# Gate row moved to the head of ScalarE's load queue, first value part placed ahead of x1's transposes, one dummy matmul pair fewer

## The chip, the core and the metric

The kernel runs on one core of one Trainium2 chip. The metric is device time in microseconds of one launch, from the runs of the kernel: three runs before the change, of which the median counts. The profile shows one further execution, taken by the hardware profiler.

## What is computed

A gated mix of a linear attention (hedgehog features) and a SwiGLU feed-forward block, both fed from the same x of 2048 tokens by 640 columns, in bf16:

```python
def reference(A_x, A_wqkv, A_w_phi, A_wo, B_x, B_w_gate, B_w_up, B_w_down, gate_w):
    def _A_ref(x, wqkv, w_phi, wo):            # 32 heads of 20 columns
        qkv = (x @ wqkv).reshape(B, S, 3, H, Dh).transpose(2, 0, 3, 1, 4)
        q, k, v = qkv[0], qkv[1], qkv[2]
        pq = jnp.einsum("bhsd,hdf->bhsf", q, w_phi)
        pk = jnp.einsum("bhsd,hdf->bhsf", k, w_phi)
        phi_q = jnp.concatenate([_softmax(pq), _softmax(-pq)], axis=-1)
        phi_k = jnp.concatenate([_softmax(pk), _softmax(-pk)], axis=-1)
        kv = jnp.einsum("bhsf,bhsd->bhfd", phi_k, v)
        z  = jnp.einsum("bhsf->bhf", phi_k)
        num = jnp.einsum("bhqf,bhfd->bhqd", phi_q, kv)
        den = jnp.einsum("bhqf,bhf->bhq", phi_q, z)[..., None] + 1e-6
        return (num / den).transpose(0, 2, 1, 3).reshape(B, S, D) @ wo
    def _B_ref(x, w_gate, w_up, w_down):
        return (_silu(x @ w_gate) * (x @ w_up)) @ w_down
    x = A_x
    g = _sigmoid((x * gate_w).sum(-1, keepdims=True))
    return g * _A_ref(x, A_wqkv, A_w_phi, A_wo) + (1 - g) * _B_ref(x, B_w_gate, B_w_up, B_w_down)
```

The part that matters here is the start: the values v = x @ wqkv[:, 1280:1920], to which the gate's column is joined (gate_w becomes the 641st column of the value weights, so that the gate's logit falls out of the same matmuls).

## The kernel before

The tokens are cut into 16 tiles of 128 (t = 0 to 15), the 640 columns of x into 5 chunks of 128. Two strings set everything: LOADS (line 33) is the order in which the transfers from HBM are issued, ORDER (line 38) the order in which the work is handed to the engines. Each word is one item, run by the table at line 952. Each engine then works through its own list in order; a wait on another engine or on a transfer is a semaphore wait that the tracker (line 145) puts in front of an instruction. An instruction that waits holds up all that stands behind it on its engine, and a transfer is issued by the engine in whose list it stands (SP or ScalarE, shown as SPq and ACTq in the profile).

The items of the head, in the names of the strings:

- x0 to x3 load the first four tiles of x as rows (128 x 640, 160 KB, into xs); XQ at line 391 gives x0 to SP and x1, x2, x3 to ScalarE.
- w0 to w4 load the five row chunks of the value weights (128 x 640 each, 160 KB, into wvg); WQ at line 392 gives w0 and w4 to ScalarE, w1, w2, w3 to SP.
- g loads the gate row gate_w as five rows of 128 into gwr (line 414, on SP). It waits for the memset that clears gwr on GpSimd (line 431).
- f0, k0 and further words load weights on SP.
- H (warm, line 511) is a pair of dummy matmuls of 128x128 on a constant, which need no data. ORDER starts with 13 of them.
- X0.0 transposes chunk 0 of x0 on TensorE into PSUM and lets VectorE copy it to xT; X0.1 does so for the other four chunks, with the copy on ScalarE. X1, X2, X3 transpose whole tiles, all copied on VectorE.
- G (gcol, line 505) turns the five gate rows into five columns on TensorE, and VectorE casts them into column 640 of wvg.
- U t.c (vpart, line 539) is chunk c of the values of tile t: two matmuls of 320 and 321 columns with wvg's chunk c, which add up over c in one PSUM pair of banks. The last, c = 4, hands the pair to ScalarE (v_out).
- h loads w_phi on ScalarE after a wait on w3.

PSUM has four pairs of banks. next_pair (line 489) gives an item the pair that was used longest ago and is not held; a pair handed out again is written only when its last reader is done. Every H, too, takes a pair. From the item I to the item N the pair 3 is out of this ring, since it collects the key-value sums.

After the head, TensorE runs value tiles (V), feature premultiplication of the weights (M), key tiles (K), key-value sums (E), query tiles (Q), feed-forward items (F), output of the attention (O) and the down projection (D).

Of the kernel before, what the change touches and what calls it, by code (L numbers as in the profile page):

```python
# [6 lines left out]
P = 128  # L7
# [23 lines left out]


LOADS = """
x0 w0 x1 g w1 x2 w2 x3 w3 w4 f0 k0 k1 t4 k2 k3 k4 k5 t5 t6 t7 t8 t9 t10 t11 t12 t13 t14 t15 q0 q1 q2 q3 q4 q5
 f1 f2
"""

ORDER = """
H0 H1 H2 H3 H4 H5 H6 H7 H8 H9 H10 H11 H12 X0.0 G X0.1 X1 h U0.0 U1.0 U0.1 X2 U1.1 U2.0 U0.2 U1.2
U2.1 X3 U2.2 U0.3 U1.3 U2.3 U0.4 U1.4 U2.4 V3 Y i4 F0.1 M0 M1 F0.2 M2 V4 M3 M4 F0.0 M5 K0 i3 K1 S0 I  # L40
P0 K3 S1 P1 F1.0 K2 V6 E0 V8 K4 S2 S3 E1 S4 K5 S5 P2 P3 V7 E2 V5 R0 K6 P4 P5 R2 E3 K7 S6 E4 V15 K8
E5 V10 S7 P6 K9 E6 R1 P7 S8 K10 S9 E7 K11 S10 V9 V11 P8 E8 K12 P9 R3 E9 P10 K13 S11 E10 K14 S12 P11
# [11 lines left out]
class _Tracker:  # L54
# [90 lines left out]
    def run(self, eng, fn, reads=(), writes=(), dma=False):  # L145
        rkeys = list(dict.fromkeys(k for a in reads for k in self.keys_of(a)))
        wkeys = list(dict.fromkeys(k for a in writes for k in self.keys_of(a)))
        need = {}

        def req(ev, raw):  # L150
            if ev is None:
                return
            s, v = ev
            if s == eng and not dma and (eng == "pe" or not raw):
                return
            if v > need.get(s, 0):
                need[s] = v

        for k in rkeys:
            for kk in self._conflicts(k):  # L160
                req(self.lastw[kk], True)
                if k[0] == "psum":
                    for s, v in self.readers[kk].items():
                        req((s, v), False)
        for k in wkeys:
            for kk in self._conflicts(k):
                req(self.lastw[kk], True)
                for s, v in self.readers[kk].items():
                    req((s, v), False)
        self._wait(eng, need)  # L170
        ins = fn()
        if dma:
            sn = "d%d" % self.ndma
            self.ndma += 1
            self._add_sem(sn)
            inc = 16
        else:
            sn, inc = eng, 1
        ins.then_inc(self.sem[sn], inc)
        self.cnt[sn] += inc  # L180
        v = self.cnt[sn]
        snap = dict(self.known[eng])
        if not dma:
            snap[sn] = max(snap.get(sn, 0), v)
        self.evknow.setdefault(sn, {})[v] = snap
        ev = (sn, v)
        for k in wkeys:
            self.lastw[k] = ev
            self.readers[k] = {}
        for k in rkeys:  # L190
            r = self.readers[k]
            if r.get(sn, 0) < v:
                r[sn] = v
        return ev


def _build(nc, A_x, A_wqkv, A_w_phi, A_wo, B_x, B_w_gate, B_w_up, B_w_down, gate_w, out):
    tr = _Tracker(nc)
    pe, act, dve, pool, sp = nc.tensor, nc.scalar, nc.vector, nc.gpsimd, nc.sync
# [3 lines left out]
    def sb(name, shape, dtype):  # L203
        t = nc.alloc_sbuf_tensor(name, list(shape), dtype)
        tr.reg(t, "sbuf", nc.lookup_mloc(t).addr)
        return t
# [94 lines left out]
    gwr = sb("gwr", [P, P], BF16)  # L301
# [72 lines left out]
    def dma(e, dst, src, transpose=False):  # L374
        eo = tr.eng[e]

        def fn():
            if transpose:
                return eo.dma_start_transpose(dst, src)
            return eo.dma_start(dst, src)  # L380
        rd = [src] if src.tensor.name in tr.base else []
        wr = [dst] if dst.tensor.name in tr.base else []
        return run(e, fn, rd, wr, dma=True)
# [9 lines left out]
    x2 = A_x[0]  # L393
# [18 lines left out]
        wv_evs.append(load_rows(WQ[c], wvg[:, c, 0:D], c, 2 * D))  # L412

    def load_gate():
        dma("sp", gwr[0:5, :], bass.AP(gate_w.tensor, gate_w.offset, [[P, 5], [1, P]]))

    def load_phi():
        tr._wait("act", dict([wv_evs[3]]))
# [527 lines left out]
    def kv_end():  # L946
# [6 lines left out]
        "H": lambda i: warm(), "i": fills, "X": xpose, "G": gcol, "U": vpart, "V": vtile,  # L953
        "M": lambda m: premult(1, m), "R": lambda m: premult(0, m),
        "K": ktile, "S": knorm, "P": kmul, "p": lambda t: kmul(t, "dve"), "E": kvtile, "x": load_x, "t": load_xt, "w": load_wv, "g": load_gate, "h": load_phi, "k": lambda m: load_wt(1, m), "q": lambda m: load_wt(0, m),
        "f": lambda i: load_ffn(FCUT[i], FCUT[i + 1]), "L": load_late_weights, "T": tail_weights, "J": gates,
        "Y": w_blocks, "I": kv_begin, "N": kv_end, "Z": z_row,
# [51 lines left out]
```

## Time and profile before

| | us |
|---|---|
| median of 3 runs | 285.62 |
| the runs | 285.57, 285.62, 285.80 |
| the profiled execution | 286.04 |
| its span, first to last instruction | 284.8 |

| engine | busy us (share of the span) | instructions |
|---|---|---|
| TensorE matmul (PE) | 281.9 (99%) | 1809 |
| TensorE weight load (PEld) | 156.8 (55%) | 1809 |
| VectorE (DVE) | 193.2 (68%) | 280 |
| ScalarE (ACT) | 139.6 (49%) | 241 |
| GpSimd (POOL) | 155.3 (55%) | 119 |

The profiled execution has 1.2 us outside its span. Busy times of the matmuls are those of a pipeline and overlap: the spacing of their starts, not the length of one, tells how fast TensorE goes. In the timelines each line has the start, the time until the group's end, the engine, the line of the kernel, the operation, output <- inputs, and the number of instructions; in brackets the idle time ahead of the first and what ended it. "ACTq" and "SPq" are the issues of transfers by ScalarE and SP. The granted clock of TensorE is 1.00 in the whole span.

### The profile page before, as it was taken

Reading aid. Unit: us, or ns where it says so; the run is one execution under the profiler, and the core shown is the slowest. Engines: PE = TensorE matmul, PEld = TensorE weight load, DVE = VectorE, ACT = ScalarE, POOL = GpSimd, SP = SyncE. Lnnn points to the kernel's source line nnn. Section 1 sums busy time; section 2 is a strip of 40 time slices with the busy share of each in tenths; the row PEclk is TensorE's granted clock in tenths of the full one; section 3 lists DMA queues with packets and bytes.
Section 4 is the critical chain, followed back from the end, with each engine's and each line's share of the span. In section 5 each row is a group of like instructions: output and inputs, shape, how many; then the busy total and the mean of one; then the engine's idle time right before and its main releaser. Section 6 shows DMA issues by size and latency. Waiting matters only on the chain.

```text
span 284.8 us, 4696 instructions
## 1 busy us (share of the span) xinstructions
PE 281.9 (99%) x1809; PEld 156.8 (55%) x1809; DVE 193.2 (68%) x280; ACT 139.6 (49%) x241; POOL 155.3 (55%) x119
## 2 busy tenths in 40 slices
PE   8999999999999999999999999999999999999997
PEld 6666777766645445445545444554544444444766
DVE  1346667784789998979999899997878355053100
ACT  2477687786755666657746764130101675001022
POOL 6276988888167859597858744463062553100100
PEclk9999999999999999999999999999999999999999
DMA  7986679200065362022330200623547520133411
GB/s 231 232 104 129 109 136 370 86 3 0 3 218 185 78 107 51 9 52 53 60 52 3 52 4 10 138 51 71 115 139 138 76 61 7 41 78 73 122 46 46
DMA packets 62085, 25.19 MB, mean 88 GB/s; under 512 B 51023, under 2 KB 61543, under 8 KB 62063
## 3 DMA queue, kind: packets, MB, share of 16 engines
q1 hardware_dynamic: 60534, 24.03, 37.7%
q10 hardware_dynamic: 1529, 0.87, 1.1%
q8 instruction: 14, 0.23, 0.4%
q14 instruction: 8, 0.07, 0.1%
HBM read 10.16 MB, written 2.63 MB: 45 GB/s over the span
## 4 chain that ended last, share of the span: by engine, by line
PE 98%; DMA 1%; DVE 0%; issue 0%
PE ps L326 97%; DMA xs<-in_A_x_dram 1%; PE ps L338 1%; DVE osb L934 0%
## 5 line engine op out<-in xcount | busy, mean ns | idle before, releaser
L354 POOL TENSOR_TENSOR hT<-hT,us 128x512 bf16<-128x512 bf16 (+1 forms) x37 | 42.9, 1167 | 43.5 <-DVE hT L358 33.2
L326 PE MATMUL ps<-xT,wg 128*128 128x512 bf16 x260 | 64.6, 379 | 0.0
L326 PE MATMUL ps<-xT,wu 128*128 128x512 bf16 x260 | 64.6, 379 | 0.0
L354 POOL TENSOR_TENSOR ph<-eq,qc 128x1320 bf16<-128x1320 bf16 x16 | 40.3, 2521 | 31.0 <-DVE qc L673 19.8
L326 PE MATMUL ps<-wqk,xT 128*128 128x320 bf16 x320 | 47.9, 299 | 0.0
L344 ACT ACTIVATE us<-ps 128x512 bf16<-128x512 f32 (+1 forms) x56 | 33.4, 597 | 22.0 <-PE ps L326 19.8
L326 PEld LDWEIGHTS ps<-xT,wu 128*128 128x128 bf16 x260 | 25.4, 98 | 30.7
L326 PEld LDWEIGHTS ps<-xT,wg 128*128 128x128 bf16 x260 | 25.0, 98 | 28.4 <-ACT oT L344 0.6
L354 POOL TENSOR_TENSOR ekr<-ekr,krec 128x1280 bf16<-128x1280 bf16 x16 | 37.3, 2358 | 5.8 <-DVE krec L368 5.8
L344 ACT ACTIVATE eq<-ps 128x640 bf16<-128x640 f32 x32 | 22.3, 703 | 32.3 <-PE ps L326 31.2
L358 DVE SCALAR_TENSOR_TENSOR hT<-hT,ps 128x512 bf16<-128x512 bf16 (+1 forms) x37 | 25.0, 681 | 19.1 <-ACT hT L344 17.5
L326 PEld LDWEIGHTS ps<-wqk,xT 128*128 128x128 bf16 x320 | 30.4, 98 | 13.3
L354 POOL TENSOR_TENSOR hx<-hx,us 128x512 bf16<-128x512 bf16 (+1 forms) x19 | 24.1, 1272 | 22.1 <-DVE hx L358 16.3
L344 ACT ACTIVATE hT<-ps 128x512 bf16<-128x512 f32 (+1 forms) x37 | 22.0, 596 | 25.0 <-PE ps L326 24.8
L326 PE MATMUL ps<-hT,wd 128*128 128x512 bf16 (+1 forms) x140 | 31.1, 379 | 0.0
L365 DVE TENSOR_REDUCE ksum<-ekr 128x64 f32<-128x1280 bf16 x16 | 23.4, 1464 | 11.0 <-ACT ekr L344 11.0
L344 ACT ACTIVATE ekr<-ps 128x640 bf16<-128x640 f32 x32 | 22.3, 703 | 6.9 <-PE ps L326 6.4
L326 PE MATMUL ps<-wvg,xT 128*128 128x320 bf16 (+1 forms) x160 | 24.7, 305 | 0.0
L365 DVE TENSOR_REDUCE qw<-ez 128x64 f32<-128x1280 bf16 x16 | 23.6, 1476 | 0.0
L365 DVE TENSOR_REDUCE qz<-eq 128x64 f32<-128x1280 bf16 x16 | 23.6, 1478 | 0.0
L354 DVE TENSOR_TENSOR ez<-eq,zb 128x1280 bf16<-128x1280 bf16 x16 | 22.9, 1449 | 0.6 <-DMA zb<-zrow 0.6
L326 PEld LDWEIGHTS ps<-hT,wd 128*128 128x128 bf16 (+1 forms) x140 | 13.0, 97 | 16.1 <-issue 1.3
(103 smaller groups left out, 291.2 us busy)
## 6 DMA issues: line engine op xcount, KB each, us to landing
wd<-in_B_w_down_dram SPq DMA_DIRECT2D x1, 2080.0 KB, 10.3
out_dram<-osb SPq DMA_DIRECT2D x2, 640.0 KB, 3.5
wg<-in_B_w_gate_dram SPq DMA_DIRECT2D x1, 1040.0 KB, 8.6
wu<-in_B_w_up_dram SPq DMA_DIRECT2D x1, 1040.0 KB, 9.8
wog<-in_A_wo_dram SPq DMA_DIRECT2D x2, 375.0 KB, 4.1
wg<-in_B_w_gate_dram SPq DMA_DIRECT2D x1, 640.0 KB, 5.0
wu<-in_B_w_up_dram SPq DMA_DIRECT2D x1, 640.0 KB, 6.3
omgb<-omgd SPq DMA_DIRECT2D x2, 256.0 KB, 4.0
```

The source lines that it names most:

```text
L326: last = pe.matmul(o, lhsT=l, rhs=r, start=st, stop=sp_, skip_group_check=sk)
L338: last = pe.transpose(o, i, ident[0:k, 0:k])
L344: return run("act", lambda: act.activation(o, i, func, scale=scale), rd, [o])
L354: return run(e, lambda: eo.tensor_tensor(o, a, b, op), [a, b], [o])
L358: return run("dve", lambda: dve.scalar_tensor_tensor(out=o, in0=a, scalar=s, in1=b, op0=op0, op1=op1), rd, [o])
L365: return run("dve", lambda: dve.tensor_reduce(o, i, AX.X, ALU.add), [i], [o])
```

## The change

The gate row is issued by ScalarE instead of SP, as the first of its transfers, ahead of w0 and x1. In ORDER the first value part U0.0 goes ahead of X1, and one of the 13 dummy pairs at the start is left out. With one pair taken less from the ring, and U0 taking its pair ahead of X1, the numbers of the PSUM pairs that the later items get are permuted.

```diff
 LOADS = """
-x0 w0 x1 g w1 x2 w2 x3 w3 w4 f0 k0 k1 t4 k2 k3 k4 k5 t5 t6 t7 t8 t9 t10 t11 t12 t13 t14 t15 q0 q1 q2 q3 q4 q5
+x0 g w0 x1 w1 x2 w2 x3 w3 w4 f0 k0 k1 t4 k2 k3 k4 k5 t5 t6 t7 t8 t9 t10 t11 t12 t13 t14 t15 q0 q1 q2 q3 q4 q5
  f1 f2
 """

 ORDER = """
-H0 H1 H2 H3 H4 H5 H6 H7 H8 H9 H10 H11 H12 X0.0 G X0.1 X1 h U0.0 U1.0 U0.1 X2 U1.1 U2.0 U0.2 U1.2
+H0 H1 H2 H3 H4 H5 H6 H7 H8 H9 H10 H11 X0.0 G X0.1 U0.0 X1 h U1.0 U0.1 X2 U1.1 U2.0 U0.2 U1.2
...
     def load_gate():
-        dma("sp", gwr[0:5, :], bass.AP(gate_w.tensor, gate_w.offset, [[P, 5], [1, P]]))
+        dma("act", gwr[0:5, :], bass.AP(gate_w.tensor, gate_w.offset, [[P, 5], [1, P]]))
```

## Prediction

> **What bounds the kernel now.** I read the page's chain first, then the timelines of the first 9 us by engine, then a table of stretches for the matmuls that read wvg.
>
> ```profile
> PE 98%; DMA 1%; DVE 0%; issue 0%
> PE ps L326 97%; DMA xs<-in_A_x_dram 1%; PE ps L338 1%; DVE osb L934 0%
> ```
>
> The chain never leaves TensorE once x0 has landed. So the time is the start of the first transpose, plus TensorE's work, plus whatever gaps and slow matmuls stand among it. Only the head can move.
>
> ```profile
> 3.04 0.74 PE L518 MATMUL ps<-const-bfloat16-1.0 128*128 128x128 bf16 x5
> 3.85 0.29 PE L338 MATMUL ps<-ident,xs 128*128 128x128 bf16 x1
> 4.12 0.19 PE L326 MATMUL ps<-ident,gwr 128*128 128x5 bf16 x1
> 4.17 1.12 PE L338 MATMUL ps<-ident,xs 128*128 128x128 bf16 x9
> 5.08 1.67 PE L326 MATMUL ps<-wvg,xT 128*128 128x320 bf16 x6
> 6.59 0.44 PE L338 MATMUL ps<-ident,xs 128*128 128x128 bf16 x5
> 6.87 1.53 PE L326 MATMUL ps<-wvg,xT 128*128 128x320 bf16 x10
> ```
>
> ```profile
> 3.85 0.10 PEld L338 LDWEIGHTS ps<-ident,xs 128*128 128x128 bf16 x1 [0.35 <-DMA xs<-in_A_x_dram]
> 4.12 0.10 PEld L326 LDWEIGHTS ps<-ident,gwr 128*128 128x128 bf16 x1 [0.16 <-DMA gwr<-in_gate_w_dram]
> ```
>
> TensorE waits twice: for x0 (the 26 dummies are spaced 107 ns, so the last one's 107 ns end near 3.57, and X0.0 starts at 3.85: 0.29 us) and for the gate row (0.16 us). After 4.12 it has no gap in the head.
>
> ```profile
> 5.08:6.42 1.34, 1.34 (x5) 0.70 (x6) 0.00 (x0) 1.00 1.05 350
> 6.87:8.23 1.36, 1.36 (x10) 0.81 (x10) 0.00 (x0) 1.00 1.09 362
> ```
>
> This is the stretch table (stretch, sum, busy and count for TensorE first, then its weight loads). In equal time 5 matmuls of 320 columns start, and later 10: 267 ns each, then 136. The granted clock column says 1.00 in both, so it doesn't show this step. The x6 group at 5.08 is cut short in its last matmul (6.42 to the next start at 6.59, 171 ns), which puts the step near 6.50 us. Before 6.50 a wait costs about half its length: what was not done at 267 ns is done later at 136 (1 - 136/267 is lost, 0.49).
>
> ```profile
> 0.80 0.41 ACTq L380 DMA_DIRECT2D wvg<-in_A_wqkv_dram  x1
> 1.24 1.43 ACTq L380 DMA_DIRECT2D xs<-in_A_x_dram  x3
> 2.70 0.45 ACTq L380 DMA_DIRECT2D wvg<-in_A_wqkv_dram  x1
> 3.19 1.28 ACT L344 ACT_TABLE_LOAD   x1 [3.19 <-issue]
> 4.79 0.60 ACT L344 ACTIVATE xT<-ps 128x512 bf16<-128x512 bf16 x1 [0.33 <-PE ps L338]
> ```
>
> ScalarE issues five loads one after another, then loads its table until 4.47, and the copy of X0.1 follows at 4.79, when its transposes are done: slack 0.32 us.
>
> ```profile
> 0.81 0.39 SPq L380 DMA_DIRECT2D xs<-in_A_x_dram  x1
> 1.26 0.36 SPq L380 DMA_DIRECT2D gwr<-in_gate_w_dram  x1
> 1.66 1.30 SPq L380 DMA_DIRECT2D wvg<-in_A_wqkv_dram  x3
> ```
>
> **The change, part by part.** Gate row at the head of ScalarE's queue: it waits for POOL's memset of gwr (0.80 to 1.00 in the timeline), so it issues near 1.05 and takes 0.36 (its SP row), with 0.03 to the next issue, as between the others. Everything queued behind it on ScalarE moves 0.65 us: w0 from 0.80 to 1.45, x1 from 1.24 to 1.89, x2 to 2.38, x3 to 2.87, w4 to 3.35, and the table load from 3.19 to 3.84. It then ends at 5.12, and the copy of X0.1 runs 5.13 to 5.73 instead of 4.79 to 5.39. Who waits for it: U0.1, which reads the copied columns, and before that U1.0, because the PSUM ring hands U1 the pair that X0 used (before the change and after it, by the order of next_pair calls). A release reaches TensorE about 0.05 us after the end (the copy that ends at 7.08 frees a weight load at 7.13). So U1.0 starts no earlier than 5.78, against 5.62 now (two 267 ns matmuls after 5.08). On SP w1, w2, w3 and the weights behind them issue 0.42 us earlier (1.66 to 1.24), which nothing needs: those land well ahead of their use.
>
> One dummy pair fewer: 24 x 107 ns from 0.84 end near 3.41 (3.57 - 0.21).
>
> x0's landing: its issue-to-landing is 3.0 us (0.81 to 3.81) with w0 beside it, which landed at 4.0 (3.2 after 0.80). The next 160 KB, x1, landed at 4.4 (3.1 after 1.24), so 160 KB are worth some 0.4 us. Without the half of w0 that went ahead of x0's last packets, X0.0 may start near 3.6. Bounds: 3.41 (the dummies' end) and 3.85 (no gain); 3.6 is the middle, taken by the 0.4 us row. The gate row, first on its ring, should land between 1.5 us after 1.05 (the shortest landing of a store on ScalarE's queue, 24 KB) and 2.9 us after (its own wait ending at 4.12, issued 1.26), so 2.6 to 3.95. I take it as hidden; at 3.95 it would still hold TensorE 0.25 us, which the later bound on U1.0 swallows.
>
> U0.0 ahead of X1: X0.0, G and X0.1 take 0.107 + 0.047 + 4 x 0.107 = 0.58, so TensorE is free at 4.18. U0.0 needs VectorE's copy and cast (at 4.18 + 0.22 and 4.35 + 0.18 now, that is 0.67 after X0.0's start, with the hop 0.72: 4.32) and w0: 1.45 + 3.2 = 4.65 by its own row, 4.4 if it is the third 160 KB to land, as x1 is now. It then runs 0.53 us, from 4.45 to 4.98, or 4.7 to 5.23. X1 needs x1: 1.89 + 3.1 = 5.0 by its own row, 1.89 + 4.1 = 6.0 by x2's, which is now issued at 1.73 and has a rival transfer on SP, as x1 will have. I take 5.3, nearer to its own row; X1 then ends at 5.85 and U1.0 starts near 5.87. With x1 at 5.0 it is 5.78, by the ScalarE copy; with 6.0 it is 6.55.
>
> Before and after, the same work stands ahead of U1.0 (X0, G, X1, U0.0). So the whole change is U1.0's start: 5.87 against 5.62, 0.25 us later (0.16 to 0.93). The earlier x0 and the vanished gate wait buy nothing past this point, since the ScalarE copy ends late whatever TensorE does. At half price that is +0.12 us (0.08 to 0.49, the part past 6.50 counted whole).
>
> The later steps keep their cover, if each landing shifts by 0.65: x2 5.8 to 6.5 (X2 then near 6.7), x3 7.0 to 7.7 (X3 8.2), w4 8.0 to 8.7 (U0.4 9.6). The permuted PSUM pairs put F1.0 on K0's pair, whose two exponentials end near 24.1, with F1.0 at 25.15: 1 us of cover.
>
> **Sum.** The profiled execution took 286.04 (284.8 of span, 1.2 around it), the runs' median is 285.62. Span 284.8 + 0.12 gives 284.92, 286.16 for a profiled run and 285.74 against the median.
>
> **The rivals.** First, the step from 267 to 136 ns comes later. TensorE's idle time between the first dummy and the step is 0.29 + 0.16 = 0.45 us now. After, it is 3.41 to 3.6, 4.18 to 4.45, 4.98 to 5.3: 0.78, with 0.95 where x1 is later. For it: 2.73 us of unbroken dummies were not enough now, so the idle parts may count. Against: 0.45 us of gaps didn't prevent the step. Price: the step stands 2.38 us behind the end of the last gap (4.12); from 5.87 that is 8.25, 1.75 us later x 0.49 = 0.86, so 286.6. If the run-up of 5.66 us (0.84 to 6.50) counts from X0.0 at 3.6, it is 9.26, 1.35 us, so 287.1. It decides as soon as the idle share before 6.50 no longer lets the step happen there. [...]
>
> Second, x1 lands as late as x2's row: U1.0 at 6.55, +0.49, and X2 may wait another 0.1 to 0.3: 286.1 to 286.4. For it: transfers are at 339 to 363 GB/s between 5 and 8 us. Against: x1 itself came in 3.1 us.
>
> Third, x0 does not land earlier at all (3.81): U0.0 and X1 then run 0.25 later, but ScalarE's copy still sets 5.78 and x1 5.87: 285.7, no change.
>
> Fourth, faster: the waits can give back at most 0.29 + 0.16 us, halved 0.22, and only if the table load does not shift. More needs the step itself to come earlier, say at 5.0: 1.5 x 0.49 = 0.73, so 285.0. Nothing in the trace speaks for it, except that one execution shows one position of the step.
>
> **How the numbers follow.** 0.2% is 0.57 us, about what a measurement can tell. Forecast 0.38 (no measurable change, its own range 285.4 to 286.1); step later 0.37 (slower, 286.5 to 287.5); late x1 0.08 (0.05 of it beyond 0.2%); no earlier x0 0.04; faster 0.13. So faster 0.13, same 0.38 + 0.03 + 0.04 = 0.45, slower 0.37 + 0.05 = 0.42. The range 285.1 to 287.5 leaves out most of the faster case and the far end of the late step.
>
> **What would show it.** In the changed profile: w0's issue near 1.45 and the table load near 3.84; X0.0 near 3.6; no wait on the gate row; gaps ahead of U0.0 and X1; U1.0 at 5.8 to 5.9, behind ScalarE's copy or x1. The step: count matmuls of 320 columns around 6.5. If they are still at 267 ns past 7 us, the first rival holds and the forecast falls; if U1.0 starts before 5.62, my reading of ScalarE's queue is wrong.

## The result, and the profile after

The changed kernel is slower: 289.58 us median of 6 runs (288.75 to 291.36) against 285.65 us for the kernel before (285.37 to 286.4). The ratio is 1.0137, 95% interval 1.0113 to 1.0161, some 3.9 us. The profiled execution took 289.47 us, with a span of 288.2 us (before: 286.04 and 284.8).

The chain of waits of the changed kernel from 0.80 us on, its first pieces in order of time (start, length, what):

```profile
0.80 0.20 POOL gwr L372
1.00 0.15 POOL ident L372
1.16 0.43 ACTq L380
1.59 0.03 issue
1.62 0.39 ACTq L380
2.01 0.03 issue
2.04 4.65 DMA xs<-in_A_x_dram
```

Before, the chain began with x0's transfer (3.0 us). Now it leads through ScalarE's issues, the gate row's and w0's, to x1, which takes 4.65 us from issue to landing. ScalarE's own timeline shows what stands there:

```profile
1.04 0.55 ACTq L380 DMA_DIRECT2D gwr<-in_gate_w_dram  x1
1.62 0.39 ACTq L380 DMA_DIRECT2D wvg<-in_A_wqkv_dram  x1
2.04 1.41 ACTq L380 DMA_DIRECT2D xs<-in_A_x_dram  x3
3.48 0.65 ACTq L380 DMA_DIRECT2D wvg<-in_A_wqkv_dram  x1
4.16 1.28 ACT L344 ACT_TABLE_LOAD   x1 [4.16 <-POOL v1x L372]
5.46 0.60 ACT L344 ACTIVATE xT<-ps 128x512 bf16<-128x512 bf16 x1
```

w0 is issued at 1.62 instead of 0.80, x1 at 2.04 instead of 1.24. TensorE's timeline of the changed kernel:

```profile
3.35 0.31 PE L338 MATMUL ps<-ident,xs 128*128 128x128 bf16 x1
3.46 0.21 PE L326 MATMUL ps<-ident,gwr 128*128 128x5 bf16 x1
3.53 0.59 PE L338 MATMUL ps<-ident,xs 128*128 128x128 bf16 x4
5.91 0.69 PE L326 MATMUL ps<-wvg,xT 128*128 128x320 bf16 x2 [1.79 <-DMA wvg<-in_A_wqkv_dram]
6.74 0.71 PE L338 MATMUL ps<-ident,xs 128*128 128x128 bf16 x5
7.34 1.25 PE L326 MATMUL ps<-wvg,xT 128*128 128x320 bf16 x4
8.39 0.74 PE L338 MATMUL ps<-ident,xs 128*128 128x128 bf16 x5
8.92 2.88 PE L326 MATMUL ps<-wvg,xT 128*128 128x320 bf16 x10
11.60 0.56 PE L338 MATMUL ps<-ident,xs 128*128 128x128 bf16 x5
```

X0.0 starts at 3.35, right behind the dummies and 0.5 us earlier than before. Then TensorE stands still for 2 us until w0 has landed, and 0.3 us more until x1 has. U1.0 starts at 7.34; before, it was 5.62. And the slow matmuls go on: ten matmuls of a value tile take from 8.92 to 11.60 (268 ns each), where before they took 1.36 us. The table of stretches for the matmuls that read wvg (stretch, sum, busy and count of TensorE, weight loads, VectorE, granted clock, share of the transfer engines, GB/s):

```profile
9.99:11.06 1.07, 1.07 (x5) 0.60 (x4) 0.00 (x0) 1.00 1.06 139
12.00:13.07 1.07, 1.07 (x8) 0.78 (x9) 0.00 (x0) 1.00 1.24 201
```

The five transposes at 11.60 take 0.39 us to the next start (0.53 when slow, 0.28 when fast), so the step from 267 to 136 ns lies near 11.83; before, near 6.50. The granted clock column says 1.00 in both rows and again doesn't show it. The clock records of the trace, which the column is made from, begin only with the step itself: at 11.823 us, and at 6.482 in the kernel before, which agrees with the spacing. Ahead of the first record the column reads 1.00.

In the profiled execution two parts add up to the whole. U1.0 starts 7.34 - 5.62 = 1.72 us later. Behind U1.0 the matmuls stay slow for 11.83 - 7.34 = 4.49 us instead of 6.50 - 5.62 = 0.88; the 3.61 us more cost half, 0.49 x 3.61 = 1.77. Together 3.49 us. TensorE's last matmul starts at 286.13 instead of 282.66, 3.47 later. Past the head nothing moved: from the first feed-forward matmul (15.26, before 11.78) to the last matmul there are 270.87 us, before 270.88. So the permuted PSUM pairs cost nothing.

### The profile page after: what moved, and what is told of

It is laid out like the page before. It is cut to its first block, busy times and chain, and to the rows that moved or that the text cites. A ratio compares the mean times of both kernels' runs of the same rounds, so it can differ in the third digit from the quotient of the medians.

```text
span 288.2 us, 4686 instructions
## 1 busy us (share of the span) xinstructions
PE 283.2 (98%) x1800; PEld 157.3 (55%) x1807; DVE 192.6 (67%) x280; ACT 139.6 (48%) x241; POOL 155.4 (54%) x119
## 4 chain that ended last, share of the span: by engine, by line
PE 97%; DMA 2%; ACTq 0%; issue 0%; POOL 0%; DVE 0%; POOLq 0%
PE ps L326 96%; DMA xs<-in_A_x_dram 2%; PE ps L338 1%; ACTq L380 0%; DVE osb L934 0%; POOL gwr L372 0%; POOL ident L372 0%; POOLq L994 0%
## 5 line engine op out<-in xcount | busy, mean ns | idle before, releaser
L326 PE MATMUL ps<-wvg,xT 128*128 128x320 bf16 (+1 forms) x160 | 26.4, 316 | 1.8 <-DMA wvg<-in_A_wqkv_dram 1.8
L354 DVE TENSOR_TENSOR ez<-eq,zb 128x1280 bf16<-128x1280 bf16 x16 | 22.3, 1408 | 1.1 <-DMA zb<-zrow 1.1
```

The source lines that it names most:

```text
L326: last = pe.matmul(o, lhsT=l, rhs=r, start=st, stop=sp_, skip_group_check=sk)
L354: return run(e, lambda: eo.tensor_tensor(o, a, b, op), [a, b], [o])
```

## The experiments

All kernels were timed beside the kernel before on the same chip; a ratio is to that kernel. Issue and landing times below are those of the trace's transfer records in the one profiled execution of each. The code below is cut to the words that change; "..." stands for what is left out.

### Which part of the change is it

e1 keeps only the gate row's move, e2 only the order on TensorE, e3 only the missing dummy pair.

```diff
# e1: after, with ORDER as before
-H0 ... H11 X0.0 G X0.1 U0.0 X1 h U1.0
+H0 ... H12 X0.0 G X0.1 X1 h U0.0 U1.0
# e2: before, with
-X0.0 G X0.1 X1 h U0.0 U1.0
+X0.0 G X0.1 U0.0 X1 h U1.0
# e3: before, with
-H0 ... H11 H12 X0.0
+H0 ... H11 X0.0
```

> Only the gate row's move to the head of ScalarE's queue, with 13 dummy pairs and X1 ahead of U0.0 as in the kernel before. Theory Q (the move delays w0 and x1, and TensorE's long gap also delays its step from 267 to 136 ns): w0 lands near 5.8 and x1 near 6.7 as in the changed kernel, TensorE has a gap of 2 us or more, time 289 to 291. Theory O (the loss comes from U0.0 being put ahead of X1): 285.5 to 286.2, as before the change.

> Only U0.0 ahead of X1, with the gate row on SP and 13 dummy pairs. Theory Q: w0 lands at 4.0 and x1 at 4.4 as before, gap of some 0.1 us for the cast, time 285.4 to 286.0. Theory O: most of the 3.9 us, 288 or more.

> Only one dummy pair fewer. Theory Q: the gap before X0.0 grows from 0.29 to 0.50 us and nothing else, 285.4 to 286.0. Rival D (the dummies hold the step in place, and a pair fewer delays it by microseconds): 286.5 or more, with 267 ns matmuls past 7 us.

e1: 290.4 us, ratio 1.0147 (1.011 to 1.0185). w0 1.64 to 5.90, x1 2.06 to 6.80, and one gap on TensorE up to 6.85:

```profile
6.85 0.71 PE L338 MATMUL ps<-ident,xs 128*128 128x128 bf16 x5 [2.52 <-DMA xs<-in_A_x_dram]
```

e2: 285.77 us, 0.9991 (0.9972 to 1.0009). e3: 285.7 us, 0.9989 (0.9971 to 1.0007). The gate row's move is the whole loss; the other two parts make no difference that can be measured. Theory O and rival D fall.

### What the slow clock adds

e4 fills the changed kernel's waits with dummy matmuls. e9 and e10 leave all transfers as in the kernel before, and only hold TensorE at U0.0 until 7.5 us, e9 idle, e10 with dummies.

```diff
# e4: after, with b(n) = n dummy matmuls into the PSUM pair of the last H
-X0.0 G X0.1 U0.0 X1 h U1.0
+X0.0 G X0.1 b18 U0.0 b3 X1 h U1.0
# e9: before, with one more memset of GpSimd and j = TensorE's wait on it
+    hold = memset("pool", hT[:, 1, 0:4, :], 0.0)
-X0.0 G X0.1 X1 h U0.0 U1.0
+X0.0 G X0.1 X1 h j U0.0 U1.0
# e10: as e9, with (b into the pair of G)
+X0.0 G X0.1 X1 h b26 j U0.0 U1.0
```

> The changed kernel with 18 dummy matmuls (1.9 us at 107 ns) between X0.1 and U0.0 and 3 between U0.0 and X1, so that TensorE is busy while it waits for w0 and x1. If the late step is made by the gaps, U1.0 stays near 7.4 and the step comes back to 6 to 8 us: 286.8 to 287.8, some 2 us less than the changed kernel. If the step's place has nothing to do with the gaps: 289 to 290, with the step still near 11.8.

> The kernel before with one wait put into TensorE's list ahead of U0.0, on an extra memset of GpSimd that ends near 7.5 us; all transfers and their order as before. So TensorE idles 2.4 us (5.08 to 7.5) with nothing else changed. Theory H (an idle stretch makes the step from 267 to 136 ns come later): step at 9.5 to 12, 288.4 to 289.8, that is 2.4 us of waiting less 0.7 for what would have been slow before 6.5, plus half of the slow time behind 7.5. Rival (the step does not care for the gap): U0.0 on runs at 136 ns, 287.2 to 287.6.

> The same wait to 7.5 us, with 26 dummy matmuls put in front of it, so that TensorE has work in most of it. Theory H: the step stays at 4.5 to 8 and the time is 287.0 to 288.0, some 1 to 2 us below the kernel with the bare gap. Rival: the same time as the bare gap.

e4: 288.4 us, ratio 1.0074 (1.0039 to 1.0108), 1.2 us below the changed kernel by the medians, and above the 286.8 to 287.8 that was expected. In its profile x1 happened to land at 8.16, later than in the changed kernel (6.69), and U1.0 started only at 8.76; the matmuls behind it were fast all the same:

```profile
5.83 0.73 PE L326 MATMUL ps<-wvg,xT 128*128 128x320 bf16 x2
6.37 0.36 PE L529 MATMUL ps<-const-bfloat16-1.0 128*128 128x128 bf16 x3
8.21 0.45 PE L338 MATMUL ps<-ident,xs 128*128 128x128 bf16 x5 [1.47 <-DMA xs<-in_A_x_dram]
8.76 0.72 PE L326 MATMUL ps<-wvg,xT 128*128 128x320 bf16 x4
```

The five transposes at 8.21 already take the fast 0.45. So in this execution the step came early, but the wait was not shorter.

e9: 289.31 us, 1.0123 (1.0106 to 1.0139). e10: 287.73 us, 1.0076 (1.0055 to 1.0098). The wait ends at 7.5 in both; the difference of 1.58 us is what TensorE did meanwhile. The stretch tables, first e9 (stretch, sum, busy and count of TensorE, granted clock, transfer share, GB/s), then e10 (with weight loads and VectorE between, matmuls on wvg only):

```profile
4.68:6.00 1.32, 0.17 (x3) 1.00 0.92 309
6.00:7.00 1.00, 0.00 (x0) 1.00 1.08 367
7.00:7.50 0.50, 0.00 (x1) 0.62 1.06 360
7.50:10.50 3.00, 3.00 (x15) 0.50 1.36 265
10.50:11.00 0.50, 0.50 (x5) 0.96 0.07 19
```

```profile
4.68:7.50 2.82, 0.01 (x1) 0.01 (x1) 0.00 (x0) 1.00 0.98 327
7.50:8.50 1.00, 0.98 (x6) 0.49 (x6) 0.00 (x0) 1.00 1.09 360
```

Here the granted clock does show it: in e9 it falls to 0.50 inside the gap (0.62 over the half microsecond before 7.50 means some 0.38 us of it, so from about 7.12) and stays there until about 10.54. In this execution the step to fast matmuls had already come by 4.4 us, and the idle stretch took it back for 3.4 us; half of that is 1.7 us. In e10 the clock stays at 1.00. All four runs of e9 read a mean granted clock of 0.994 over the kernel, as such a fall gives, and all four of e10 read 1.000. Theory H holds, in this form: here idle time cost twice, as waiting and as slow matmuls afterwards.

The column shows a fall in three profiles, and in each it reads 0.50 for about 3.4 us. By the shares of the stretches in which the falls begin and end, they run from 7.12 to 10.54 in e9, from 7.37 to 10.78 in e13 (0.84 over 6.26 to 7.90, 0.51 over 10.00 to 10.80) and from 7.18 to 10.60 in e7 (0.94 over 6.32 to 7.30, 0.95 over 10.50 to 11.50).

What sets the place of the step in the head isn't shown. In the changed kernel it came 5.08 us after the last wait for a transfer had ended (6.74 to 11.82), in the kernel before 2.36 us after (4.12 to 6.48). In e9, whose head has the loads and the order of the kernel before up to the wait, it came by 4.4 us. Its place differs from execution to execution: the size of the loss in one execution is in part luck.

How much idle time brings a fall isn't settled by these runs. In e7 one followed a wait of 1.45 us, some 0.86 us after the wait's end (6.32 to 7.18):

```profile
6.32 0.45 PE L338 MATMUL ps<-ident,xs 128*128 128x128 bf16 x5 [1.45 <-DMA xs<-in_A_x_dram]
```

```profile
6.32:7.30 0.98, 0.88 (x8) 0.94 1.05 342
7.30:8.30 1.00, 1.00 (x9) 0.50 1.05 366
```

Behind the wait of 1.47 us in e4, and behind one of 1.77 us in e11 below, the matmuls stayed fast.

### Why w0 and x1 land so late

The prediction let a load that is issued 0.65 us later land 0.65 us later, by its own row. e11 tests that in the kernel before, with nothing moved but the start of ScalarE's issues, by 0.38 us. e5 to e8 vary the two queues of the changed kernel, and e13 takes SP's loads away from beside w0.

```diff
# e11: before, with a = ScalarE waits for GpSimd's 2nd memset
-x0 w0 x1 g w1
+x0 a w0 x1 g w1
# e5: after, with the gate row on SP and a = ScalarE waits for GpSimd's 3rd operation
-x0 g w0 x1 w1
+x0 g a w0 x1 w1
# e6: after, with y = a second gate row load on SP, into a scratch tile
+x0 y g w0 x1 w1
# e7: after, with
+x0 w0 g x1 w1
# e8: after, with z = 16 rows of x on ScalarE, into a scratch tile
+x0 z g w0 x1 w1
# e13: after, with a = SP waits for GpSimd's 9th operation (until 3.5 us)
+x0 g w0 x1 a w1
```

> The changed kernel with the gate row back on SP, behind x0, so SP's issues stand as before the change; ScalarE's first load w0 is only held back, by a wait on GpSimd's identity, to about 1.7 us (1.62 in the changed kernel, 0.80 before). Theory L (a late start of ScalarE's loads is enough: their first packets then stall both queues alone, behind x0): w0 lands at 5.3 to 6.0, 288.5 to 291. Theory C (SP's w1 and w2, issued 0.4 us earlier, take the transfer engines from w0): w0 lands at 4.4 to 4.9, 285.8 to 286.8. Theory S (the five small rows at the head of ScalarE's queue do it): as C, 285.8 to 286.8.

> The changed kernel with a second small load on SP behind x0 (the gate row once more, into a scratch tile that nobody reads in time), so that w1, w2, w3 issue at their times of before (1.66, 2.06, 2.53) while ScalarE's queue stays as changed. Theory C: w0 lands at 4.4 to 4.9, 286 to 287. Theories L and S: w0 still at 5.3 to 6.0, 288.5 to 291.

> The changed kernel with w0 first and the gate row second on ScalarE's queue. w0 issues at 0.80 again, x1 near 1.7. Theory L: w0 lands near 4.0 as before, the gate row by 4.2, x1 at 4.6 to 5.2, and time 285.4 to 286.4. Theory S (small rows anywhere ahead of x1 hold the ring): x1 at 6 or later, 287.5 or more.

> The changed kernel with one more load ahead of the gate row on ScalarE's queue: 16 rows of x (20 KB) into a tile not in use yet, issued at 0.80 with no wait. w0 is then issued near 1.8, later still. Theory L in its sharper form (the first packets of a queue are slow on each transfer engine, and the stall falls beside x0's own when the queue starts at 0.80): the stall near 3.0 to 3.7 goes, w0 lands at 4.5 to 5.0, 286.3 to 287.5. If only the time of issue counts: w0 at 5.8 or later, 289 to 291.

> The kernel before, all as it was, but ScalarE's first load held back by a wait on GpSimd's second memset, so that w0 issues near 1.2 instead of 0.80 and x1 near 1.6 instead of 1.24. If a load keeps its 3.2 us from issue to landing (as the prediction had it): w0 4.4, x1 4.7, 285.6 to 286.2. If loads issued by about 1.3 land in the first wave and the later ones only at 5 to 6 us: w0 by 4.5, x1 at 5.0 to 6.3, a gap of 0.5 to 1.5 us ahead of X1, 286.3 to 288.5.

> The changed kernel with SP's loads behind x0 (w1 and all that follow) held back until about 3.5 us, so that w0, issued at 1.6 on ScalarE, has the transfer engines to itself behind x0. If w0 is late because it shares the engines with SP's loads: it lands by 4.4 (its own 3.2 us of before, or less). If a load issued at 1.6 starts slowly whatever runs beside it: 5.0 or later. The total time says little here, since w1 comes late on purpose: 287 to 291.

| kernel | w0 issued, landed | x1 | w1 | median us | ratio (interval) |
|---|---|---|---|---|---|
| before | 0.80, 4.00 | 1.24, 4.38 | 1.66, 4.77 | 285.65 | 1 |
| after | 1.62, 5.78 | 2.04, 6.69 | 1.26, 3.49 | 289.58 | 1.0137 (1.0113 to 1.0161) |
| e5 | 1.70, 5.22 | 2.13, 5.94 | 1.66, 4.98 | 287.76 | 1.0068 (1.0046 to 1.0089) |
| e6 | 1.64, 5.27 | 2.04, 6.01 | 1.66, 5.06 | 289.5 | 1.0112 (1.0046 to 1.0178) |
| e7 | 0.80, 3.92 | 1.86, 6.28 | 1.26, 4.33 | 288.42 | 1.0078 (1.004 to 1.0116) |
| e8 | 1.86, 6.25 | 2.25, 7.12 | 1.26, 3.61 | 288.75 | 1.0112 (1.0085 to 1.0139) |
| e11 | 1.18, 3.54 | 1.60, 5.89 | 1.68, 5.69 | 288.1 | 1.0065 (1.0035 to 1.0095) |
| e13 | 1.63, 4.41 | 2.03, 4.87 | 3.50, 7.85 | 289.13 | 1.0096 (1.006 to 1.0133) |

e11 is the clearest. x1 is issued 0.36 us later than before and lands 1.51 us later; TensorE waits 1.77 us for it:

```profile
3.75 0.42 PE L338 MATMUL ps<-ident,xs 128*128 128x128 bf16 x4
5.94 0.45 PE L338 MATMUL ps<-ident,xs 128*128 128x128 bf16 x5 [1.77 <-DMA xs<-in_A_x_dram]
```

This profile is of the fastest of e11's six runs, 286.47 us; the others took 287.72 to 288.57. In it the step to fast matmuls came before 3.9 us, and the matmuls behind the wait were fast. So the trace shows the late landing and the wait, but not where the other five runs lost more.

A landing does not simply move with its issue. In all kernels of this table, what was issued by about 1.3 us landed by 4.4 us, from either queue; what was issued at 1.6 to 2.3 us, with other loads beside it, landed between 4.77 and 7.12. (Of these three loads only w1 was issued as late as that in the kernel before. It landed at 4.77 there, and in e2 and e3, which leave the loads as they were, at 6.01 and 5.55.) The edge is not a sharp one: with the changed kernel's loads w1, issued at 1.25, landed at 4.53 in e4, and in e12 below x1, issued at 1.26, landed at 4.86.

e5 and e6 fall between the ranges of their theories (w0 at 5.22 and 5.27): w0 still lands 1.2 us past its time of before, with the gate row on ScalarE's queue or without it, and in e11 x1 is late with no gate row on that queue at all. So theory S falls. Whether putting back SP's start helps isn't shown: with the changed kernel's own loads w0 landed at 5.78, at 5.90 (e1) and at 5.00 (e4), and of the two times only e5's lies clearly below the changed kernel's. Neither theory L nor theory C alone fits all of this. e7 saves w0 and loses x1 instead, which was issued at 1.86. e8 missed: waking ScalarE's queue early with 16 rows brought no sooner landing.

e13 says what w0 meets. Issued at 1.63, without SP's loads beside it, it lands at 4.41, not at 5.78 (5.00 in e4, the earliest with SP's loads beside it). The issue rows of w0 (size, us to landing), changed kernel first, then e13:

```profile
wvg<-in_A_wqkv_dram ACTq DMA_DIRECT2D x1, 160.0 KB, 4.2
```

```profile
wvg<-in_A_wqkv_dram ACTq DMA_DIRECT2D x1, 160.0 KB, 2.8
```

So in this trace most of the delay is the company of w1, w2 and w3 on SP. That the change moved them 0.4 us ahead can't be all of it, since e5 and e6 put them back and w0 landed at 5.2 and 5.3. (e13's own time says little: it then waits for w1, to 7.85.) It is more than a share of a fixed rate, though. The stretch from 3 to 4 us, in the kernel before, the changed kernel and e13 (last columns: granted clock, transfer share, GB/s):

```profile
3.00:4.00 1.00, 0.92 (x9) 0.61 (x6) 0.00 (x0) 0.81 (x1) 0.94 (x3) 1.00 1.07 384
```

```profile
3.00:4.00 1.00, 1.00 (x12) 0.85 (x9) 0.29 (x2) 0.00 (x0) 0.94 (x3) 1.00 0.80 141
```

```profile
3.00:4.00 1.00, 1.00 (x12) 0.85 (x9) 0.29 (x2) 0.05 (x1) 0.94 (x3) 1.00 0.86 269
```

In the changed kernel both queues start a load behind their first ones, and the engines move 141 GB/s (137 in e1 and 224 in e4, with the same loads); in e13 only ScalarE's queue has loads left, and they move 269; in the kernel before, 384. Why the rate falls there stays open; no run here separates the causes.

### Can the gate row leave SP's queue at no cost

e14 keeps the gate row on ScalarE, but puts w0 on SP behind x0, so that all four urgent loads are issued by 1.27 us. e12 gives the row to GpSimd.

```diff
# e14: before, with the gate row on ScalarE and
-WQ = ["act", "sp", "sp", "sp", "act"]
+WQ = ["sp", "sp", "sp", "sp", "act"]
-x0 w0 x1 g w1
+x0 x1 w0 g w1
# e12: before, with the gate row issued right behind its memset
-x0 w0 x1 g w1
+x0 w0 x1 w1
-        dma("sp", gwr[0:5, :], ...
+        dma("pool", gwr[0:5, :], ...
```

> The kernel before with the gate row on ScalarE's queue, as in the change, but with nothing urgent behind it: ScalarE issues x1 at 0.80 and the gate row at 1.26, SP issues x0 at 0.81 and w0 at 1.26. If the whole loss is urgent loads issued past about 1.3 us: all four land by 4.5, no gap over 0.2 us after X0.0, and 285.3 to 286.0, no change against the kernel before. If the gate row on ScalarE's queue is itself the harm: 287 or more.

> The kernel before with the gate row issued by GpSimd, right behind the memset of its tile, so that neither SP nor ScalarE has it in its queue: x0 and w0 at 0.80, x1 and w1 near 1.25. If the gate row can be moved for free when no other load is delayed: TensorE's 0.16 us wait for it goes, w1 lands by 4.5, 285.3 to 285.8. If GpSimd's issue is slow: a longer wait ahead of G, 285.8 to 287.

e14: 285.89 us, ratio 0.9988 (0.996 to 1.0017). x0 lands at 3.49, x1 3.68, the gate row 3.77, w0 4.06. Its TensorE timeline has no wait over 0.15 us up to U1.0 (U0.1 then waits 0.24 us for w1, at 6.04):

```profile
3.57 0.31 PE L338 MATMUL ps<-ident,xs 128*128 128x128 bf16 x1
3.82 0.19 PE L326 MATMUL ps<-ident,gwr 128*128 128x5 bf16 x1
3.87 1.12 PE L338 MATMUL ps<-ident,xs 128*128 128x128 bf16 x9
4.78 1.75 PE L326 MATMUL ps<-wvg,xT 128*128 128x320 bf16 x6
```

So the row on ScalarE's queue is harmless where nothing urgent stands behind it. U0.0 starts 0.3 us earlier than before, among slow matmuls, which no timing here can tell from nothing. No version tried beats the kernel before.

e12: 288.15 us, ratio 1.0084 (1.0064 to 1.0104), past the 287 that was expected at most. The row, issued at 1.34, landed at 5.05, and G waited for it:

```profile
1.34 0.70 POOL L380 DMA_DIRECT2D gwr<-in_gate_w_dram  x1 [0.33 <-POOL gwr L372]
```

```profile
5.10 0.18 PE L326 MATMUL ps<-ident,gwr 128*128 128x5 bf16 x1 [0.96 <-DMA gwr<-in_gate_w_dram]
```

This, too, is the profile of the fastest run, 286.28 us; the other four took 288.01 to 288.37. Two more things changed with it: w1 is issued at 1.26 instead of 1.66, and GpSimd's identity comes 1.1 us later. No run separates these from the row's late landing.

## Why the prediction was wrong

The forecast of no measurable change, 285.74, was wrong, and so was the range: 289.58 lies past its upper end of 287.5.

- What bounds the kernel, and that only the head can move: right, to 0.01 us behind the head.
- The queue on ScalarE: right in kind. The gate row's issue took 0.55, not 0.36, so everything behind it moved 0.82, not 0.65.
- x0 earlier, the gate row hidden, the dummy pair free: right. x0 landed 0.7 us earlier (predicted 0.25), and X0.0 started at the dummies' end. As the prediction said, that bought nothing.
- The failing step is "w0: 1.45 + 3.2 = 4.65 by its own row" and "x1: 1.89 + 3.1 = 5.0 by its own row". They carry an issue-to-landing time over to another issue time. w0 took 4.2 and x1 4.65, so they landed 1.1 and 1.7 us past these sums. The rows that told of it were used for x1's upper end alone: in the kernel before, loads of equal size took 3.0 to 3.2 us when issued by 1.7, and 4.1 to 5.3 when issued later. e11 shows the late landing with nothing moved but ScalarE's issues, e13 that the company of SP's loads makes most of it. Why that company costs so much stays open.
- SP's loads 0.42 us earlier, "which nothing needs": right that nothing needs it, but what it costs others was not asked. With SP's loads out of the way (e13) w0 lands 1.4 us sooner; that the 0.42 us alone matter isn't shown (e5, e6).
- "5.87 against 5.62, 0.25 us later (0.16 to 0.93)" for U1.0: it was 1.72 later. ScalarE's copy, which was to bind, ended at 6.06 and was long done.
- The late step was the first rival, and it happened; its price, worked out from U1.0 at 5.87 (8.25 to 9.26), was too small, as the gaps were 2.4 us and not 0.78. Measured 11.83. Rival and long wait came together, from one cause, and the text priced them one at a time.
- The rival's own range reached to 287.5, past both of its prices (286.6 and 287.1); no run shows a term for that. The runs of the changed kernel took 288.75 to 291.36, with the step at 11.82 in the profiled one. That idle time ahead of the step makes it come later was the rival's premise: with the waits filled, the step came before 8.21 in e4's profile, but how much idle time moves it by how much isn't shown. The profiles have slow matmuls from a wait on in e9 (0.50 for 3.4 us), and none behind waits of 1.47 and 1.77 us in e4 and e11.

## What to carry to other kernels

In these traces a transfer's time from issue to landing changed with its time of issue and with the loads beside it, at equal size (w0's 160 KB took 2.4 us in e11, 2.8 in e13 and 4.2 in the changed kernel): before a small load is put ahead of urgent ones, list what each queue has issued by when, and look in the same trace for loads of equal size at the later place. When a head is bound by landings, keep all urgent loads in the first round of issues over both queues and put the small or late ones behind them; e14 does so and loses nothing. And price a gap on TensorE as more than the wait: the work behind it ran at a clock of 0.50 for some 3.4 us in e9, and dummies in the gap saved 1.58 us in e10.

## What the runs showed of the hardware

- Delaying the start of one queue's loads by 0.38 us made the kernel slower by a ratio of 1.0065 (1.0035 to 1.0095), some 1.9 us (e11). In the profiled execution, the fastest, one urgent transfer landed 1.51 us later.
- The granted clock column doesn't show the slow matmuls of a kernel's start (1.00 at 267 ns in the changed kernel up to 11.82 us), but does show a later fall (0.50, 3.4 us, in e9).
- The granted clock fell to 0.50 in e7, e9 and e13 and stayed there for about 3.4 us in each (7.18 to 10.60, 7.12 to 10.54, 7.37 to 10.78).
- A load of 1.2 KB issued by GpSimd took 3.7 us to land (1.34 to 5.05), where the same row at the head of ScalarE's queue took 2.1 (1.04 to 3.13, changed kernel).
